# Clustered attention and two feed-forward parts on one core: a new order of the attention steps, with products and sums visited together

## The chip, the cores and the metric
The kernel runs on 1 core of one Trainium2 chip. The metric is the device time of one execution in microseconds (us). PE is the matrix engine, PEld its loading of weights, DVE, ACT and POOL the vector, scalar and GpSimd engines, SP the engine that issues the DMAs here.

## What is computed
```python
# one core computes all of it; B, H, S, D = 2, 8, 768, 64; 16 clusters
q_assign = np.argmax(np.einsum('bhsd,hcd->bhsc', q_n, c_n), axis=-1)   # rows and centroids of length 1
k_assign = np.argmax(np.einsum('bhsd,hcd->bhsc', k_n, c_n), axis=-1)
mask = q_assign[:, :, :, None] == k_assign[:, :, None, :]
scores = np.where(mask, scale * np.matmul(q, k.transpose(0, 1, 3, 2)), -1000000000.0)
attn = np.exp(scores - np.max(scores, axis=-1, keepdims=True))
attn = attn / (np.sum(attn, axis=-1, keepdims=True) + 1e-09)
x = np.matmul(attn, v)              # then laid out as (B*S, H*D) = (1536, 512)
h = x @ w_in                        # first feed-forward part, 2048 wide
x = (np.maximum(h, 0.0) + np.log1p(np.exp(-np.abs(h)))) @ w_out
h = x @ w_in2                       # second one, with a ratio of two polynomials of h
x = (P(h) / (Q(h) + 1e-6)) @ w_out2
```
Where no key has a query's cluster, all scores of that row are equal and the result is the mean of v; the kernel carries such absent rows by a flag.

## The kernel before
The eight pairs of heads (NP = 8) are done in eight steps, `step(j)`, after a lead-in. A step interleaves work of four pairs. Of pair j it does the 24 score products (`scores`, tile `st`: two matrix instructions each, exponential on ACT into `et`, additions of those tiles on POOL into `ea`) and the products with v (`av`: per block of 128 keys two float32 instructions for each half n of the 768 queries, collected in the PSUM banks `av0` and `av1`; in block 0 also one product with `gr` and `gv` for the absent rows). Of pair j+1 it does 24 products for the row maxima (`maxes`, tile `mxs`, each reduced on DVE), then `max_rows1` and `max_rows2` (L293 to L314): DVE takes the larger of two maxima, clips it into `nm` in three operations (the negated maximum, and twice the flag of an absent row), PE transposes `nm` into `nt`, ACT copies it into `nr`, and two DMAs bring its rows into `qt` and `gr`; also the column sums of v (`vsum1` on DVE, `vsum2` on PE). Of pair j+2 it does the transposes of q and k with their split into a high and a low part, the products with the centroids (`dots`, tile `dt`), the one-hot of the nearest centroid (`onehot`, L233 to L252: on DVE a max, a compare, a multiplication on POOL, a min, a compare) and its transposes (`mask_rows`, tile `ot`), whose rows go to `qt` and `kt` by DMA. Of pair j-1 it does the sums of the exponentials (`sums`, tile `sm`, by a product with ones; ACT copies each into SBUF) and `finish` (logarithm and exponential on ACT for the reciprocal, three DVE operations, the high part by ACT and the low part by POOL into `xh` and `xl`).

PSUM has eight banks: `av0`, `av1`, and six that `bank` (L63 to L67) hands out in turn to all other tiles. A product into a bank waits until the tile that had it six calls earlier has been read.

What sets the order is a table, `P["AT"]` (L22): score product i has position i, every other piece of work a position in the table, and `step` writes the pieces in the order of the positions (L695 on). `later` puts off a part of a piece by some places. The lead-in has its own table. In the last step the weights of the feed-forward parts begin to arrive and are decoded on DVE (`decode_w`, four pieces per block, run by `run_pieces`). Behind the steps the last pair's sums are made and finished, and the feed-forward parts follow in units of 512 rows by 128 of the 2048 columns, with four pieces of decoding per unit.

## Time and profile before
| | us |
|---|---|
| median of three runs | 907.64 |
| the three runs | 907.53, 913.1, 907.64 |
| profiled execution, its time | 907.15 |
| profiled execution, its span | 905.4 |
| PE busy | 838.6 (93%) |
| DVE busy | 645.0 (71%) |
| ACT busy | 442.0 (49%) |
| POOL busy | 168.3 (19%) |

The span is what the profile covers, from the first to the last instruction; the execution's own time lies 1.75 us above it. The mean granted clock of PE over the span is 0.962 of full speed. Busy shares are means over parts with different limits, so the stages are read one by one below.

### The profile page before, as it was taken

The numbers are of one execution on the slowest core, as the hardware profiler recorded it, in microseconds if no ns is written. First come the engines' busy times: TensorE is split into PE (matmuls) and PEld (weight loads), VectorE is DVE, ScalarE is ACT, GpSimd is POOL, SyncE is SP. The second block draws the span as 40 slices with busy tenths as digits, with TensorE's granted clock in tenths as the row PEclk, the third lists the DMA queues.
The fourth block names the chain that finished last, engine by engine and source line by source line (L and its number), as shares of the span: only waits on it lengthen the run. The fifth ranks groups of instructions, "written<-read, shape, count | busy, mean of one in ns | idle before, by whom it ended". The sixth has DMA issues, their size and how long they took to land.

```text
span 905.4 us, 10141 instructions
## 1 busy us (share of the span) xinstructions
PE 838.6 (93%) x3721; PEld 612.2 (68%) x3721; DVE 645.0 (71%) x955; ACT 442.0 (49%) x772; POOL 168.3 (19%) x110
## 2 busy tenths in 40 slices
PE   6698898988989967999999999999899999999997
PEld 6565465654645425777888888876678878887885
DVE  6776877868768586887201137887999888888886
ACT  3145354553545534334322233335667776776764
POOL 2063745738458320000000000000000000000000
PEclk9598999999999979999999999999899999999999
DMA  9776364563620729000000005552000010001001
GB/s 195 172 162 146 62 140 89 116 145 77 141 54 12 303 86 401 0 1 1 1 0 1 1 23 209 186 186 93 1 1 1 0 47 1 1 0 47 1 1 47
DMA packets 44290, 71.37 MB, mean 79 GB/s; under 512 B 28320, under 2 KB 30672, under 8 KB 40144
## 3 DMA queue, kind: packets, MB, share of 16 engines
q1 hardware_dynamic: 44240, 70.72, 27.8%
q8 instruction: 29, 0.48, 0.2%
q14 instruction: 21, 0.17, 0.1%
HBM read 43.03 MB, written 3.15 MB: 51 GB/s over the span
## 4 chain that ended last, share of the span: by engine, by line
PE 57%; DVE 28%; ACT 10%; issue 3%; DMA 2%; SPq 0%; DVEq 0%; ACTq 0%
PE av L377 7%; PE h L513 6%; PE h L514 6%; PE h L515 6%; DVE w L474 4%; DVE w L480 4%; PE yp L589 4%; PE yp L590 4%; PE st L351 4%; PE yp L588 4%; PE mxs L283 3%; ACT w L484 3%; PE st L352 3%; DVE w L468 2%; PE yp L585 2%
## 5 line engine op out<-in xcount | busy, mean ns | idle before, releaser
L513 PE MATMUL h<-xh,w 128*128 128x512 f32 x384 | 151.1, 393 | 2.9 <-ACT last L410 2.9
L514 PE MATMUL h<-xl,w 128*128 128x512 f32 x384 | 150.9, 393 | 0.0
L515 PE MATMUL h<-xh,w 128*128 128x512 f32 x384 | 150.8, 393 | 0.0
L356 ACT ACTIVATE et<-st 128x384 f32<-128x384 f32 x192 | 88.6, 488 | 69.3 <-PE st L352 66.0
L289 DVE TENSOR_REDUCE mx<-mxs 128x1 f32<-128x384 f32 x192 | 98.1, 551 | 29.6 <-PE mxs L283 29.5
L362 POOL TENSOR_TENSOR ea<-ea,et 128x768 f32<-128x768 f32 x60 | 109.5, 1844 | 30.7 <-ACT et L356 30.7
L569 DVE TENSOR_TENSOR gl<-y,gh 128x512 fp32r<-128x512 f32 x48 | 33.2, 692 | 96.1 <-ACT gh L561 96.1
L377 PE MATMUL av<-et,vr 128*64 128x384 f32 x384 | 94.0, 565 | 5.8 <-ACT et L356 5.7
L484 ACT CAST w<-w 128x1024 fp32r<-128x1024 f32 x32 | 33.6, 1049 | 124.5 <-DVE w L480 124.5
L513 PEld LDWEIGHTS h<-xh,w 128*128 128x128 f32 x384 | 72.2, 188 | 20.0 <-ACT last L410 3.6
L515 PEld LDWEIGHTS h<-xh,w 128*128 128x128 f32 x384 | 72.2, 188 | 16.5
L514 PEld LDWEIGHTS h<-xl,w 128*128 128x128 f32 x384 | 72.2, 188 | 16.4
L588 PE MATMUL yp<-w,gh 128*128 128x512 f32 x192 | 76.9, 400 | 6.5 <-ACT gh L563 6.3
L585 PE MATMUL yp<-gl,w 128*128 128x512 f32 x192 | 77.6, 404 | 4.1 <-DVE gl L569 4.1
L584 PE MATMUL yp<-gh,w 128*128 128x512 f32 x192 | 76.8, 400 | 3.8 <-ACT gh L561 3.8
L589 PE MATMUL yp<-w,gl 128*128 128x512 f32 x192 | 77.5, 404 | 2.0 <-DVE gl L571 1.9
L590 PE MATMUL yp<-w,gh 128*128 128x512 f32 x192 | 76.3, 397 | 0.0
L586 PE MATMUL yp<-gh,w 128*128 128x512 f32 x192 | 75.5, 393 | 0.0
L351 PE MATMUL st<-qt,kk 128*128 128x384 f32 x192 | 73.6, 383 | 0.0
L526 ACT ACTIVATE y<-h 128x512 f32<-128x512 f32 x48 | 28.5, 594 | 81.9 <-PE h L515 81.8
L283 PE MATMUL mxs<-kt,qt 80*128 80x384 f32 x192 | 63.0, 386 | 5.6 <-DMA kt<-mr 5.6
L352 PE MATMUL st<-qt,kt 81*128 81x384 f32 x192 | 65.9, 343 | 0.0
(140 smaller groups left out, 1452.2 us busy)
## 6 DMA issues: line engine op xcount, KB each, us to landing
w<-in_moe_w SPq DMA_DIRECT2D x32, 1024.0 KB
qt<-hiq SPq DMA_DIRECT2D x16, 384.0 KB
kk<-hik SPq DMA_DIRECT2D x32, 192.0 KB
qraw<-in_q SPq DMA_DIRECT2D x8, 384.0 KB
kraw<-in_k SPq DMA_DIRECT2D x8, 384.0 KB
vr<-in_v SPq DMA_DIRECT2D x8, 384.0 KB
qt<-loq SPq DMA_DIRECT2D x16, 192.0 KB
kt<-hik SPq DMA_DIRECT2D x16, 192.0 KB
```

The lines of the kernel that those rows point to most:

```text
L289: nc.vector.tensor_reduce(out=nm_t[j][:, h, i, n:n + 1], in_=t[:, 0:HS], axis=AX.X, op=ALU.max)
L351: nc.tensor.matmul(t[:, 0:HS], lhsT=KK[j % 2][:, h, c], rhs=QT[j % 3][:, 0, h, r], start=True, stop=False)
L352: nc.tensor.matmul(t[:, 0:HS], lhsT=KT[j % 3][0:65 + C, 1, h, c], rhs=QT[j % 3][0:65 + C, 1, h, r], start=False, stop=True)
L362: eng.tensor_tensor(out=ea[j, h], in0=et[j, 0, h] if first else ea[j, h], in1=e, op=ALU.add)
L377: nc.tensor.matmul(t[64 * h:64 * h + 64, 0:HS], lhsT=VR[j % 2][:, h, kt, :], rhs=et[j, kt, h][:, n, :], start=False, stop=kt == NT - 1,)
L513: nc.tensor.matmul(t, lhsT=wh[:, kk, :], rhs=h, start=kk == 0, stop=False)
L514: nc.tensor.matmul(t, lhsT=wh[:, kk, :], rhs=l, start=False, stop=False)
L515: nc.tensor.matmul(t, lhsT=wl[:, kk, :], rhs=h, start=False, stop=kk == KD - 1)
L585: nc.tensor.matmul(t, lhsT=wh[:, s], rhs=gl, start=False, stop=False)
L588: nc.tensor.matmul(t, lhsT=gh[:, s], rhs=wh, start=first, stop=False)
L589: nc.tensor.matmul(t, lhsT=gl[:, s], rhs=wh, start=False, stop=False)
L590: nc.tensor.matmul(t, lhsT=gh[:, s], rhs=wl, start=False, stop=last)
```

## The change
All steps but the lead-in's get a new table of positions.

- **Joint visits.** `av` is called once per block of keys, for both halves of the queries, as eight or four instructions in a row. The visit to block 0 also makes the sums of the pair before. Its position is 6.6 (before, the two halves had 0.33 and 7.58 behind a block's scores); the last block's is 2.6 in the next step.
- **Sums' banks.** The two `sm` banks are put on the list `held`, which `bank` passes over, until a position behind `finish`. The copies by ACT go for all but the last pair: `finish` now reads and writes the bank itself, adds 1e-9 as a bias of the logarithm and inside its first DVE operation, and stands in three parts at the positions `F`.
- **Maxima.** `max_rows1` is one reduction, which writes the unclipped maxima twice into a tile `mf` that stays (columns 0 to 11 and 32 to 43). PE transposes 44 columns, and DVE clips 12 rows each for the maximum and for the flag out of PSUM. The rows of `gr` are written by two DMAs in place of one.
- **Other positions.** The transposes of q and k stand later, `dots` at 13.8 and 14.8 (before 7.73 and 8.27), `mask_rows` at 19.8 and 20.8 (12.45 and 13.87), `vsum1` at 16.8 (14.74), `vsum2` at 22.5 (46.03), the reading of q and k at 7.5 (16.92). Tiles `ds` and `mr` get buffers of their own.
- **Weights.** Seven and not eight blocks have their place before attention ends, working tiles move to the other pool, and the fourth piece of a decoding is put behind the first of the next.
- **End of attention.** Both halves of `finish` go part by part.

```diff
...
+    AT=dict(MX=[round(0.5 + 0.7 * x, 2) for x in range(24)], AV=6.6, AVP=2.6, T=[-0.5, -0.4, 3.7, 4.7], D=[13.8, 14.8],
+            OT=[19.8, 20.8], F=[8.3, 10.2, 16.4], V1=16.8, V2=22.5, MR=[16.7, 18.6], LK=5.48, LD=7.5, LV=3.2,
+            DE=[15.9, 19.9, 23.9], LAST=8.6, FREE=2.6),
...
-    nbank = [0]
+    nbank, held = [0], []
     def bank(nm):
         nbank[0] += 1
+        while nbank[0] % 6 in held:
...
+    MF = [ap_.tile([128, 2, 32], F32, name=f"mf{s}") for s in range(2)]
...
-        return er_.tile(shape, dt, tag={"ds": "kraw", "mr": "qraw"}.get(tag, tag), name=tag, bufs=bufs)
+        return er_.tile(shape, dt, tag=tag, name=tag, bufs=bufs)
...
     def max_rows1(j):
-        m = nm_t.pop(j)
+        m = nm_t.pop(j).rearrange("p h i n -> p (h i) n")
         assert ("mx", j) in ok
-        nm = nm_p.tile([128, 3, 2 * NT], F32, tag="nm", name="nm", bufs=2)
-        mf = nm_p.tile([128, 2 * NT], F32, tag="mf", name="mf", bufs=2)
-        nc.vector.tensor_reduce(out=mf, in_=m.rearrange("p h i n -> p (h i) n"), axis=AX.X, op=ALU.max)
-        nc.vector.tensor_scalar(nm[:, 0, :], mf, -CLIP, -1.0, op0=ALU.max, op1=ALU.mult)
-        for x in (1, 2):
-            nc.vector.tensor_scalar(nm[:, x, :], mf, -CLIP, None, op0=ALU.is_le)
-        nr_t[j] = nm
+        nc.vector.tensor_reduce(
+            out=MF[j % 2][:, :, 0:2 * NT], in_=m.unsqueeze(1).to_broadcast([128, 2, 2 * NT, 2]), axis=AX.X, op=ALU.max
+        )
     def max_rows2(j):
-        nm = nr_t.pop(j)
         assert j < 2 or ("sm", j - 2) in ok
         ok.add(("mr", j))
         t = bank("nt")
-        nc.tensor.transpose(t[0:36, 0:128], nm.rearrange("p a b -> p (a b)"), ident)
-        nr = nm_p.tile([36, 128], F32R, tag="nr", name="nr", bufs=2)
-        nc.scalar.copy(nr, t[0:36, 0:128])
-        move(QT[j % 3][64 + C:65 + C, 1, :, :], nr[0:12, :])
-        move(GR[j % 2], nr[12:36, :])
+        w = 32 + 2 * NT
+        nc.tensor.transpose(t[0:w, 0:128], MF[j % 2].rearrange("p a b -> p (a b)")[:, 0:w], ident)
+        nr = nm_p.tile([w, 128], F32R, tag="nr", name="nr", bufs=2)
+        nc.vector.tensor_scalar(nr[0:2 * NT, :], t[0:2 * NT, 0:128], -CLIP, -1.0, op0=ALU.max, op1=ALU.mult)
+        nc.vector.tensor_scalar(nr[32:w, :], t[32:w, 0:128], -CLIP, None, op0=ALU.is_le)
+        move(QT[j % 3][64 + C:65 + C, 1, :, :], nr[0:2 * NT, :])
+        for x in range(2):
+            move(GR[j % 2][2 * x:2 * x + 2], nr[32:w, :])
...
-    def av(j, kt, n):
-        if kt == 0:
-            av_t[j, n] = ps1.tile([128, 512], F32, tag=f"av{n}", name="av")
-        t = av_t[j, n]
-        r = slice(n * HS, (n + 1) * HS)
+    def av(j, kt, p=None):
+        if p is not None:
+            for n in range(2):
+                sm_t[p, n] = bank("sm")
+                held.append(nbank[0] % 6)
+                absent(sm_t[p, n], p, n, g768[64 * (p % 2):64 * (p % 2) + 4, :])
         if kt == 0:
             assert ("gv", j) in ok
-            nc.tensor.matmul(t[:, 0:HS], lhsT=GV[j % 2], rhs=GR[j % 2][:, r], start=True, stop=False)
-        for h in range(2):
-            nc.tensor.matmul(
-                t[64 * h:64 * h + 64, 0:HS], lhsT=VR[j % 2][:, h, kt, :], rhs=et[j, kt, h][:, n, :],
-                start=False, stop=kt == NT - 1,
-            )
-        if n == 1 and kt == NT - 1:
+            for n in range(2):
+                av_t[j, n] = ps1.tile([128, 512], F32, tag=f"av{n}", name="av")
+                absent(av_t[j, n], j, n, GV[j % 2])
+        if p is not None:
+            sums(p)
+        for n in range(2):
+            for h in range(2):
+                nc.tensor.matmul(
+                    av_t[j, n][64 * h:64 * h + 64, 0:HS], lhsT=VR[j % 2][:, h, kt, :], rhs=et[j, kt, h][:, n, :],
+                    start=False, stop=kt == NT - 1,
+                )
+        if kt == NT - 1:
             ok.add(("av", j))
-        if n == 1 and kt != 0:
+        if kt != 0:
             for h in range(2):
                 et.pop((j, kt, h))
         if kt == NT - 1 and j < NP - 1:
-            evac_av(j, n, nm_p.tile([128, HS], F32, tag=f"avs{n}", name="avs"))
+            for n in range(2):
+                evac_av(j, n, nm_p.tile([128, HS], F32, tag=f"avs{n}", name="avs"))
+    def absent(t, j, n, g):
+        nc.tensor.matmul(t[:, 0:HS], lhsT=g, rhs=GR[j % 2][:, n * HS:(n + 1) * HS], start=True, stop=False)
     def evac_av(j, n, t):
         avs_t[j, n] = t
         nc.scalar.activation(out=t, in_=av_t.pop((j, n))[:, 0:HS], func=AF.Copy, scale=-1.0)
-    def sums(j, n):
-        t = bank("sm")
-        r = slice(n * HS, (n + 1) * HS)
-        p = 64 * (j % 2)
-        nc.tensor.matmul(t[:, 0:HS], lhsT=g768[p:p + 4, :], rhs=GR[j % 2][:, r], start=True, stop=False)
-        for h in range(2):
-            nc.tensor.matmul(
-                t[64 * h:64 * h + 64, 0:HS], lhsT=ones, rhs=ea[j, h][:, n, :], start=False, stop=True
-            )
-        if n == 1:
-            ea.pop((j, 0)), ea.pop((j, 1))
-            ok.add(("sm", j))
-        sm_t[j, n] = t
-        if j < NP - 1:
-            evac_sums(j, n, nm_p.tile([128, HS], F32, tag="sm", name="sm", bufs=2))
+    def sums(j):
+        for n in range(2):
+            for h in range(2):
+                nc.tensor.matmul(
+                    sm_t[j, n][64 * h:64 * h + 64, 0:HS], lhsT=ones, rhs=ea[j, h][:, n, :], start=False, stop=True
+                )
+        ea.pop((j, 0)), ea.pop((j, 1))
+        ok.add(("sm", j))
     def evac_sums(j, n, sm):
-        nc.scalar.activation(out=sm, in_=sm_t[j, n][:, 0:HS], func=AF.Identity, bias=eps9)
+        nc.scalar.activation(out=sm, in_=sm_t[j, n][:, 0:HS], func=AF.Copy)
         sm_t[j, n] = sm
-    def finish(j, n, d1=P["DF"][0], d2=P["DF"][1]):
-        sm = sm_t.pop((j, n))
-        r0 = fin.tile([128, HS], F32, tag="r0", name="r0")
-        nc.scalar.activation(out=r0, in_=sm, func=AF.Ln)
-        nc.scalar.activation(out=r0, in_=r0, func=AF.Exp, scale=-1.0)
-        r = slice(j // PB * S + n * HS, j // PB * S + (n + 1) * HS)
-        hi, lo = xh[j % PB][:, r], xl[j % PB][:, r]
-        a = avs_t.pop((j, n))
-        def rest():
-            nc.vector.tensor_tensor(out=sm, in0=sm, in1=r0, op=ALU.mult)
-            nc.vector.scalar_tensor_tensor(out=r0, in0=sm, scalar=-2.0, in1=r0, op0=ALU.add, op1=ALU.mult)
-            nc.vector.tensor_tensor(out=a, in0=a, in1=r0, op=ALU.mult)
-        def last():
+    r_t = {}
+    def finish(j, n, part):
+        sm = sm_t[j, n] if j == NP - 1 else sm_t[j, n][:, 0:HS]
+        if part == 0:
+            r_t[j, n] = fin.tile([128, HS], F32, tag="r0", name="r0", bufs=2)
+        r0, a = r_t[j, n], avs_t[j, n]
+        if part == 0:
+            nc.scalar.activation(out=r0, in_=sm, func=AF.Ln, bias=eps9)
+            nc.scalar.activation(out=r0, in_=r0, func=AF.Exp, scale=-1.0)
+        elif part == 1:
+            nc.vector.scalar_tensor_tensor(out=sm, in0=sm, scalar=EPS, in1=r0, op0=ALU.add, op1=ALU.mult)
+            nc.vector.scalar_tensor_tensor(out=sm, in0=sm, scalar=-2.0, in1=r0, op0=ALU.add, op1=ALU.mult)
+            nc.vector.tensor_tensor(out=a, in0=a, in1=sm, op=ALU.mult)
+        else:
+            r = slice(j // PB * S + n * HS, j // PB * S + (n + 1) * HS)
+            hi, lo = xh[j % PB][:, r], xl[j % PB][:, r]
             nc.scalar.copy(hi, a)
             nc.gpsimd.tensor_tensor(out=lo, in0=a, in1=hi.bitcast(F32), op=ALU.subtract)
-        later(d1, rest)
-        later(d2, last)
+            sm_t.pop((j, n)), r_t.pop((j, n)), avs_t.pop((j, n))
...
+    NA = 7
...
-        return pools["wa" if s < 8 else "wb"].tile([128, 2 * NW], dt, tag=f"w{s}", name=f"w{s}")
+        return pools["wa" if s < NA else "wb"].tile([128, 2 * NW], dt, tag=f"w{s}", name=f"w{s}")
...
-        pieces.extend(((f, c), x) for x in (first, second, third, fourth))
+        key = (f, c)
+        pieces.extend([(key, first)] + tail + [(key, second), (key, third)])
+        tail[:] = [(key, fourth)]
     def run_pieces(n=0, upto=None):
-        while pieces and (n > 0 or upto and pieces[0][0] <= upto):
-            pieces.pop(0)[1]()
+        while True:
+            todo = pieces or tail
+            if not todo or not (n > 0 or upto and todo[0][0] <= upto):
+                return
+            todo.pop(0)[1]()
...
-        return pools["wb"].tile([128, TB], dt, tag=nm, name=nm, bufs=bufs)
+        return pools["wa"].tile([128, TB], dt, tag=nm, name=nm, bufs=bufs)
...
+            put(at["AVP"], lambda: av(prev, NT - 1), prev is not None)
+            for kt in range(NT - 1):
+                put(4 * kt + at["AV" if m is not None else "LAST"], lambda kt=kt: av(main, kt, prev if kt == 0 else None))
             for n in range(2):
-                put(at["AVP"][n], lambda n=n: av(prev, NT - 1, n), prev is not None)
-                for kt in range(NT - 1):
-                    put(4 * kt + 4 + at["AV"][n], lambda kt=kt, n=n: av(main, kt, n))
                 for w in range(2):
                     put(at["T"][2 * w + n], lambda w=w, n=n: transposes(p, "qk"[w], n), p is not None and p > 2)
                 put(at["D"][n], lambda n=n: dots(p, n), p is not None)
                 put(at["OT"][n], lambda n=n: mask_rows(p, n), p is not None)
-                put(at["SM"][n], lambda n=n: (sums(prev, n), finish(prev, n)), prev is not None)
+                for x in range(3):
+                    put(at["F"][x] + n + (0 if m is not None else at["LAST"] - at["AV"]), lambda n=n, x=x: finish(prev, n, x), prev is not None)
+                put(at["F"][1] + n + at["FREE"], lambda: held.pop(0), prev is not None)
...
-        for c in range(8):
+        for c in range(NA):
             stage_w(0, c)
         step(NP - 1)
-        av(NP - 1, NT - 1, 0)
-        av(NP - 1, NT - 1, 1)
+        av(NP - 1, NT - 1)
         for n in range(2):
-            sums(NP - 1, n)
+            sm_t[NP - 1, n] = bank("sm")
+            absent(sm_t[NP - 1, n], NP - 1, n, g768[64 * ((NP - 1) % 2):64 * ((NP - 1) % 2) + 4, :])
+        sums(NP - 1)
...
-        for n in range(2):
-            finish(NP - 1, n, 1, 2)
-            tick(), tick()
-        for c in range(8, KF - 2):
+        for x in range(3):
+            for n in range(2):
+                finish(NP - 1, n, x)
+        for c in range(NA, KF - 2):
```

In the order of PE, a middle step (score products of pair 3) around the sums of the pair before; `st` are score products, `mxs` those of the maxima, `sm` the sums, `av` the products with v. Before:
```order
L397 MATMUL sm<-gr,g_76 128x384
L399 MATMUL sm<-ea,ones 64x384 x2
L351 MATMUL st<-qt_100,kk_107 128x384
L352 MATMUL st<-qt_100,kt_103 128x384
L283 MATMUL mxs<-kt_104,qt_101 128x384
L351 MATMUL st<-qt_100,kk_107 128x384
L352 MATMUL st<-qt_100,kt_103 128x384
L375 MATMUL av<-gr,gv 128x384
L377 MATMUL av<-et,vr_109 64x384 x2
L351 MATMUL st<-qt_100,kk_107 128x384
L352 MATMUL st<-qt_100,kt_103 128x384
L397 MATMUL sm<-gr,g_76 128x384
```
After, the joint visit of the same step:
```order
L290 MATMUL mxs<-kt_104,qt_101 128x384
L402 MATMUL sm<-gr,g_76 128x384 x2
L402 MATMUL av<-gr,gv 128x384 x2
L411 MATMUL sm<-ea,ones 64x384 x4
L388 MATMUL av<-et,vr_109 64x384 x4
L290 MATMUL mxs<-kt_104,qt_101 128x384
L355 MATMUL st<-qt_100,kk_107 128x384
L356 MATMUL st<-qt_100,kt_103 128x384
```
The three visits to the sums and to `av`, which stood between score products, have become one stretch of twelve instructions with the sums of both halves in it.

In the order of DVE, behind the products with the centroids; `ds` and `dmx` belong to the one-hot, `mx` and `mf` to the maxima, `vs` to the column sums of v. Before:
```order
L227 TENSOR_REDUCE ds<-dt 128x192 x2
L241 TENSOR_REDUCE dmx<-ds 128x24
L242 TENSOR_TENSOR ds<-ds,dmx 128x384
L289 TENSOR_REDUCE mx<-mxs 128x1 x3
L246 TENSOR_REDUCE dmx<-ds 128x24
L249 TENSOR_TENSOR ds<-iota,dmx 128x384
L289 TENSOR_REDUCE mx<-mxs 128x1 x4
L320 TENSOR_REDUCE vs<-vr_108 128x128
```
After, in the same step:
```order
L234 TENSOR_REDUCE ds<-dt 128x192
L296 TENSOR_REDUCE mx<-mxs 128x1
L234 TENSOR_REDUCE ds<-dt 128x192
L248 TENSOR_REDUCE dmx<-ds 128x24
L249 TENSOR_TENSOR ds<-ds,dmx 128x384
L296 TENSOR_REDUCE mx<-mxs 128x1 x3
L302 TENSOR_REDUCE mf_112<-mx 128x2x12
L324 TENSOR_REDUCE vs<-vr_108 128x128
L253 TENSOR_REDUCE dmx<-ds 128x24
L256 TENSOR_TENSOR ds<-iota,dmx 128x384
L313 TENSOR_SCALAR nr<-nt 12x128
L314 TENSOR_SCALAR nr<-nt 12x128
```
The reduction into `mf` and the column sums of v stand ahead of the last two operations of the one-hot, and the two clips, now on `nr`, behind them.

In the order of PE, the end of a step; `nt` is the transpose of the maxima, `tp` that of q and k, `vt` the column sums, `ot` the transposes of the one-hot. Before:
```order
L351 MATMUL st<-qt_102,kk_106 128x384
L352 MATMUL st<-qt_102,kt_105 128x384
L351 MATMUL st<-qt_102,kk_106 128x384
L352 MATMUL st<-qt_102,kt_105 128x384
L377 MATMUL av<-et,vr_108 64x384 x2
L309 MATMUL nt<-ident,nm 36x128
L377 MATMUL av<-et,vr_108 64x384 x2
L327 MATMUL vt<-vs,ones 2x128
L164 MATMUL tp<-ident,qraw 128x128 x6
L377 MATMUL av<-et,vr_108 64x384 x4
```
After, in the same part of the step:
```order
L355 MATMUL st<-qt_100,kk_107 128x384
L356 MATMUL st<-qt_100,kt_103 128x384
L388 MATMUL av<-et,vr_109 64x384 x4
L311 MATMUL nt<-ident,mf_112 44x128
L355 MATMUL st<-qt_100,kk_107 128x384
L356 MATMUL st<-qt_100,kt_103 128x384
L267 LDWEIGHTS ds
L267 MATMUL ot<-ident_70,ds 64x128
L267 LDWEIGHTS ds
L267 MATMUL ot<-ident_70,ds 64x128
```
The transpose `nt`, which stood between products with v behind the last score product, stands behind a whole visit and ahead of the transposes `ot`, with a score product between.

## Rows read from the trace of the kernel before

**Rows 1.** Windows: us, busy time by engine, granted clock, DMA share, GB/s.
```profile
153.00:191.00 38.00, 34.54 (x179) 21.00 (x177) 28.82 (x49) 18.93 (x42) 21.72 (x13) 0.95 0.52 112
427.00:546.00 119.00, 118.78 (x515) 96.34 (x514) 25.44 (x35) 32.60 (x54) 0.00 (x0) 1.00 0.04 14
```
**Rows 2.** Waits: engine and line that waited, for whom, us in total, times, longest.
```profile
PE nt L309 <- DVE nm L301: 21.2, 8, 2.7
PE ot L260 <- DVE ds L249: 4.2, 5, 0.9
```
**Rows 3.** Timeline from 183 to 188 us: start, duration, engine, line, out<-in, idle before.
```profile
183.59 3.56 POOL L362 TENSOR_TENSOR ea<-ea,et 128x768 f32<-128x768 f32 x2 [1.20 <-ACT et L356]
183.94 1.49 DVE L299 TENSOR_SCALAR nm<-mf 128x12 f32<-128x12 f32 x1
185.34 1.85 DVE L301 TENSOR_SCALAR nm<-mf 128x12 f32<-128x12 f32 x2
187.24 0.29 PE L309 MATMUL nt<-ident,nm 128*36 128x128 f32 x1 [2.63 <-DVE nm L301]
```
**Rows 4.** Timeline of DVE at the end of the lead-in, the first clip.
```profile
40.37 0.17 DVE L299 TENSOR_SCALAR nm<-mf 128x12 f32<-128x12 f32 x1
```
**Rows 5.** Windows of 2 to 6 us, each just behind a hole of PE.
```profile
72.00:78.00 6.00, 5.75 (x19) 2.39 (x21) 2.30 (x7) 1.58 (x4) 0.16 (x1) 0.50 0.02 5
188.00:191.50 3.50, 3.50 (x15) 1.76 (x14) 1.95 (x6) 0.98 (x2) 0.00 (x0) 0.52 0.02 5
332.00:334.00 2.00, 2.00 (x7) 0.82 (x6) 2.00 (x3) 0.17 (x1) 0.00 (x0) 0.50 0.00 0
340.00:342.00 2.00, 2.00 (x9) 1.64 (x10) 0.57 (x2) 1.33 (x3) 0.00 (x0) 1.00 1.04 426
```
**Rows 6.** Timeline of PE in a middle step, score products and products with v.
```profile
196.20 0.34 PE L351 MATMUL st<-qt,kk 128*128 128x384 f32 x1
196.38 0.33 PE L352 MATMUL st<-qt,kt 81*128 81x384 f32 x1
196.64 0.43 PE L375 MATMUL av<-gr,gv 4*128 4x384 f32 x1
197.00 0.87 PE L377 MATMUL av<-et,vr 128*64 128x384 f32 x4
197.80 0.44 PE L351 MATMUL st<-qt,kk 128*128 128x384 f32 x1
198.08 0.34 PE L352 MATMUL st<-qt,kt 81*128 81x384 f32 x1
```
**Rows 7.** Timelines of DVE, PE and ACT in the last step and behind it.
```profile
323.25 2.30 DVE L468 TENSOR_SCALAR w<-w 128x1024 uint32<-128x1024 uint32 x1
331.09 3.58 PE L377 MATMUL av<-et,vr 128*64 128x384 f32 x8 [2.16 <-ACT et L356]
339.97 0.50 PE L513 MATMUL h<-xh,w 128*128 128x512 f32 x1 [2.93 <-ACT last L410]
346.75 0.51 ACT L429 CAST xh<-last 128x384 fp32r<-128x384 f32 x1 [2.09 <-DVE last L426]
```
**Rows 8.** Timeline of DVE behind the second products with the centroids, a middle step.
```profile
205.56 0.55 DVE L241 TENSOR_REDUCE dmx<-ds 128x24 f32<-128x384 f32 x1
206.15 0.56 DVE L242 TENSOR_TENSOR ds<-ds,dmx 128x384 f32<-128x384 f32 x1
206.63 1.48 DVE L289 TENSOR_REDUCE mx<-mxs 128x1 f32<-128x384 f32 x3
208.02 0.54 DVE L246 TENSOR_REDUCE dmx<-ds 128x24 f32<-128x384 f32 x1
208.59 1.44 DVE L249 TENSOR_TENSOR ds<-iota,dmx 128x384 bf16<-128x384 f32 x1
```
**Rows 9.** Lines: the column sum of v on DVE; busy time, mean ns, idle before.
```profile
L320 DVE TENSOR_REDUCE vs<-vr 128x128 f32<-128x768 f32 x8 | 12.1, 1510 | 0.0
```
**Rows 10.** One line's instructions, the one-hot: shortest, median and longest in ns.
```profile
L249 DVE TENSOR_TENSOR ds<-iota,dmx x8: 557/1436/1448, 18.6 to 246.4; 128x384 bf16<-128x384 f32 x8
```

More of the change, by code (lines that the diff above doesn't have):

```diff
@@ L19 @@
 CLIP = float(2.0 ** 60)
-P = dict(LAG=6, I0=2, L=[0, 2, 3, 4], FIN=[8, 12], ORD='gi s0 ev e4 e3 de e2 e1 s1 go', DT=1, DD=1, DO=8, DF=[4, 13],
-    AT=dict(MX=[0.52, 3.72, 5.26, 5.34, 8.39, 9.39, 10.39, 12.2, 12.32, 13.64, 14.24, 14.86, 15.36, 16.01, 16.53, 17.43, 18.38, 19.03, 19.11, 19.77, 20.02, 20.08, 20.12, 21.64], AV=[0.33, 7.58], AVP=[-3.07, -1.36], T=[-6.73, -5.56, -0.01, 0.51], D=[7.73, 8.27], OT=[12.45, 13.87], SM=[2.92, 5.06], V1=14.74, V2=46.03, MR=[21.65, 26.91], LK=5.48, LD=16.92, LV=-1.25, DE=[15.9, 19.9, 23.9], SP=[19.95, 23.95]),
+P = dict(DT=1, DD=1, DO=8,
+    AT=dict(MX=[round(0.5 + 0.7 * x, 2) for x in range(24)], AV=6.6, AVP=2.6, T=[-0.5, -0.4, 3.7, 4.7], D=[13.8, 14.8],
+            OT=[19.8, 20.8], F=[8.3, 10.2, 16.4], V1=16.8, V2=22.5, MR=[16.7, 18.6], LK=5.48, LD=7.5, LV=3.2,
+            DE=[15.9, 19.9, 23.9], LAST=8.6, FREE=2.6),
     LEAD=dict(CT=-3.26, T0=[0, 1, 2, 3], D0=[3.54, 4.41], T1=[5.03, 6.13, 7.03, 7.96], O0=[9.69, 10.33], D1=[9.44, 10.44], O1=[16.53, 19.95], T2=[42.38, 43.88, 44.05, 46.48], MX=[12.1, 13.1, 14.1, 15.08, 16.1, 17.1, 18.1, 19.1, 20.1, 21.1, 22.1, 23.1, 24.1, 25.1, 26.1, 27.1, 28.1, 29.1, 30.1, 31.1, 32.1, 33.1, 34.1, 35.1], C2=5.33, LK=15.05, LD=0.75, V1=9.2, V2=10.7, MR=[36.3, 36.83], DO=[4, 0], MV=[16.86, 22.72]))
@@ L62, in clustered_attention_two_ffns @@
     ps1 = ctx.enter_context(tc.tile_pool(name="ps1", bufs=1, space=bass.MemoryType.PSUM))
-    nbank = [0]
+    nbank, held = [0], []
     def bank(nm):
         nbank[0] += 1
+        while nbank[0] % 6 in held:
+            nbank[0] += 1
         return ps1.tile([128, 512], F32, tag=f"s{nbank[0] % 6}", name=nm)
@@ L208, in clustered_attention_two_ffns @@
     ds_t, oh_t = {}, {}
+    EPS = 1e-9
     NX = HH * 4
@@ L450, in stage_w @@
         nc.sync.dma_start(out=wt[f, c], in_=(w1, w2)[f][c].bitcast(U32))
-    pieces = []
+    pieces, tail = [], []
     def decode_w(f, c):
@@ L620, in clustered_attention_two_ffns @@
         eps9 = const.tile([128, 1], F32, name="eps9")
-        nc.vector.memset(eps9, 1e-9)
+        nc.vector.memset(eps9, EPS)
         one = const.tile([128, 1], F32, name="one")
@@ L639, in clustered_attention_two_ffns @@
         nc.gpsimd.memset(gv.bitcast(F32), 0.0)
+        for s in range(2):
+            nc.gpsimd.memset(MF[s], 0.0)
         csq = er_.tile([128, D], F32, name="csq")
```

1 line of the change is left out of this document (removed).

## The prediction
> **What bounds the kernel now.** I read the stages first. In a middle attention step the matrix engine (PE) is busy for 34.54 of 38 us and its granted clock is only 0.95, while DVE has 28.8 us of work and ACT 18.9; in the feed-forward part that follows PE is busy 118.78 of 119 us at clock 1.00 [rows 1]. So the attention steps are PE's, with holes in them, and the next thing to read is who makes the holes. The list of waits names two: PE waits 21.2 us in 8 places for the clipped maxima before their transpose `nt`, and 4.2 us in 5 places for the one-hot masks before `ot` [rows 2]. The timeline of the end of a step shows the first of them: after the last maximum DVE clips 12 numbers per partition in three small operations that take 1.49 and 1.85 us (for two), and PE stands still for 2.63 us [rows 3]. In the lead-in, where POOL has nothing to do, the first of these operations took 0.17 us [rows 4]; in the step a pair of POOL additions ran beside them and ended at 183.59 + 3.56 = 187.15, 0.04 before they did. [...] A step therefore loses 2.65 + 0.84 us of waiting (21.2 / 8 and 4.2 / 5) and 3.5 x 0.48 = 1.7 us of clock.
>
> The profiled execution took 907.15 us, its span is 905.4; the median of the three runs is 907.64. I sum against 907.15 and take the result as it stands.
>
> **What goes.** (a) The transpose of the maxima now stands behind a joint visit of eight product instructions and takes the raw maxima; on DVE only one reduction (some 0.2 us, after the 0.17 of rows 4) lies between the last maximum and it. The clips follow it, on 12 rows of 128 out of PSUM; no row shows them, the nearest are the clip's own 0.17 alone and 1.49 beside POOL. I take 0.3 each, and at either price they stand behind what PE waits for. So the wait goes in steps 0 to 6: 7 x 2.65 = 18.5 us. In the lead-in PE waits for the queue of maxima, not for the clips, so there it stays, less some 0.3.
> (b) The half clock behind it: 3.0 us in step 0 (72 to 78), 1.7 in each of six other steps, 13.2 us.
> (c) PE work. A score product starts 0.18 us after the one before; going into a float32 product costs 0.26, the first score behind it 0.28, and the single mask product of 4 rows 0.36 [rows 6]. Each float32 instruction takes 0.20 (four in 0.80). The number of them is unchanged. By the order, a step had 13 stretches of float32 work and now has 11 (products that already stood beside transposes gain nothing): 2 x 0.19; and of four single mask products three no longer stand alone: 3 x 0.18. That is 0.9 us a step, 6.5 in seven.
> (d) At the end of attention ACT did logarithm and exponential of the second half only after it had waited for DVE's first half; its last copy waited 2.09 us for DVE [rows 7]. Now both halves go ahead: 1.9 us, and the feed-forward part starts that much earlier.
> Together 40.1 us.
>
> At nothing I count: the dropped copies of the sums and of `nr` on ACT (an engine busy 18.93 of 38 us), the reads of q and k issued earlier, one more small transfer per step, and the new list of weight pieces: four pieces are run per unit as before, and DVE's order there is the same. ACT's idle half and DMA queues busy 0.52 of the stage [rows 1] cover these; if that fails the price is some tenths of a us per step.
>
> **What comes.** (e) The sums' two banks leave the rotation of six from the joint visit until DVE has finished with each. I count from the start of that visit. PE: 4 mask products and 16 float32 instructions, 4.1 us; then to the 20th maximum 11 max products, 7 score pairs and a visit of eight, 1.96 + 2.5 + 1.8 = 6.3, in all 10.4. DVE gets the first of these maxima at 4.5 and must do seven maxima at 0.49 (three in 1.48 [rows 8]) and six operations of the finish at 0.57: 4.5 + 6.9 = 11.4. The 20th maximum uses the second sums' bank, so PE waits 1.0; I add 0.7 for the dots behind it, which wait for the 17th maximum, and for smaller waits of the kind. I take 1.7 us, between 0 (if DVE overlaps better) and 2.5. The finish reads and writes PSUM in place; that form has no row. The bounds are the 0.56 of the compare and the 1.44 of the one-hot [rows 8], both two-operand operations of its size; I take 0.57.
> In steps 1 to 6: 10.2 us.
> (f) The masks. Behind the reduction of the second dots DVE had max, compare, three maxima, min, one-hot: 205.56 to 210.03 [rows 8], and PE waited 0.84. Now the dots come eight positions later in the step, and between the three maxima and the min stand the reduction of the maxima and the column sum of v, 1.51 us [rows 9]. The new chain: 0.55 + 0.55 + 0.56 + 1.48 + 0.2 + 1.51 + 0.54 + (0.56 to 1.45) = 5.95 to 6.84, with the small gaps 6.0 to 6.9, starting 0.3 behind PE's last dot. PE has five score pairs, three max products, one visit of eight, `nt`: 1.8 + 0.5 + 1.8 + 0.4 = 4.5. So PE waits 1.9 to 2.8 us at `ot`. There is one thing more: the compare starts about 1.5 us after the last dot, and POOL's addition of the scores just released (1.78 us, half of the pair of rows 3) about 1.4 after it. The one-hot, of the same kind, took 0.56 at best, in the lead-in, and 1.45 at most, beside a POOL addition [rows 10]; the compare of rows 8 had none beside it. If it is held like that, the chain grows by 1.6 and PE waits 3.8 in two parts (at `nt`, then at `ot`). I take 3.3 us, nearer to the second; the ends are 1.9 and 4.4. Six steps, less the 4.2 us of today: 15.6 us.
> [...]
> (g) A hole of this size lowers the clock or not: those at `nt` did, one of 2.16 did (0.50 behind it), one of 2.93 did not (1.00) [rows 5, 7]; those of 0.84 did not, since 3.5 us at 0.52 alone make the mean of 0.95 in 38 us. I take three in four: 6 x 0.75 x 1.7 = 7.7 us.
> (h) In the last step POOL's two subtractions of the finish move from before the weight decode into it; a decoding operation that ran beside POOL took 2.30 us [rows 7]. I take one such operation as the cost, against a start some 1.1 earlier: 1.2, bounds -1 and 3.
> Together 34.7 us.
>
> **Sum.** 907.15 - 40.1 + 34.7 = 901.7, say 902 us. The wait moves from the maxima to the masks, and most of the gain is spent there.
>
> **Rivals.** *The wait at the masks stays short and the clock full.* [...] Against it: the column sum's 1.5 us is certain, and 2.16 was enough once. Then (e) 1.0 x 6, (f) 2.0 x 6 - 4.2, (g) and (h) nothing: 13.8 added, 881 us.
> *Slower: the compare is held behind POOL in each masked step.* Place: DVE's compare behind the second dots. It costs the top of (f), 4.4 x 6 - 4.2 = 22.2; the split wait leaves PE so little to do that the clock stays low as long as after 72 us, 3.0 x 6 = 18; the late DVE stretches (e) to 2.5, 15.0, and (h) is 2.3: 57.5 added, 924.5 us. It decides from the point where (e), (f) and (g) add 6.7 us per step. For it: POOL is first by 0.1 us in my count. Against it: only one of seven holes had the long low clock.
> [...]
>
> **How the numbers follow.** A measurement of this kernel can tell about 1%, 9 us, from no change. My forecast (waits traded, 895 to 909) has 0.50, the first rival 0.34, the slower one 0.14, and 0.02 is left. Faster by over 1% (under 898) takes the first rival and the lower end of mine: 0.43. Within 1%: 0.43. Slower: 0.14. The range reaches from the first rival's 882 to 913, which leaves out most of the slower one and the last of the faster.
>
> **What would show it.** Right: no wait of PE at `nt` in the waits beyond some tenths, or 1.6 us where the compare is held; a wait of 2 to 4 us at `ot` behind the one-hot in six places; DVE busy without a gap from the joint visit to the second finish, and max products or dots waiting about 1 us there for DVE; the clock at 0.5 for some 3 us behind `ot`; a step with no masks to wait for (the seventh) shorter by some 4 us. Wrong: `ot` waits under 1.5 us and the clock of a middle step is 1.00 (then the first rival), or a middle step is over 39 us (then the slower one); or the feed-forward part, which I leave untouched, differs by more than 3 us.

## Result and the profile after

The changed kernel is slower: a median of 924.46 us in 20 executions (913.55 to 931.68) against 908.53 in 20 of the kernel before, and a ratio of 1.011 between comparable executions (interval 1.008 to 1.014); the comparisons leave disturbed runs out. The forecast was 902, with a range up to 913. The profiled execution took 921.84 us, 14.7 more than the one before.

First the stages, as windows from one step's first score product to the next one's (columns as in [rows 1]). Of the kernel before, a middle step and the last:

```profile
117.02:154.84 37.82, 34.32 (x181) 20.98 (x179) 28.83 (x49) 18.99 (x42) 21.72 (x13) 0.95 0.51 112
299.46:339.97 40.51, 31.79 (x120) 15.10 (x118) 27.89 (x24) 18.77 (x40) 11.82 (x6) 0.86 0.55 221
```

Of the changed kernel, the same two, and the step without masks:

```profile
121.52:162.70 41.18, 36.54 (x181) 23.03 (x179) 25.86 (x48) 17.62 (x39) 21.30 (x13) 0.88 0.50 104
283.38:312.15 28.77, 27.75 (x137) 17.10 (x137) 19.06 (x37) 14.82 (x32) 17.05 (x11) 0.93 0.16 42
312.15:354.84 42.69, 28.41 (x128) 15.33 (x127) 28.52 (x26) 18.38 (x40) 16.65 (x9) 0.88 0.48 192
```

A middle step is 3.4 us longer. PE stands still for 41.18 - 36.54 = 4.64 us in place of 3.50, 1.1 more. The clock costs 41.18 x 0.12 = 4.9 us in place of 37.82 x 0.05 = 1.9, 3.0 more. What is left, PE's work at full clock, falls from 32.4 to 31.6. So the joint visits do save work (0.8 us), holes change little, and the clock takes more than three times what the visits save. Steps 1 to 5 together are 14.9 us longer; by the same reckoning the clock (0.88, in step 3 0.91; before 0.95) costs 23.2 us in them in place of 9.4, 13.8 more. Step 0 is 0.9 shorter, the step without masks 3.5 shorter, the last 2.2 longer, and the lead-in 2.1. The feed-forward part begins 14.87 us later (354.84 against 339.97) and then takes as long as before.

The waits of PE (columns as in [rows 2]), of the changed kernel:

```profile
PE ot L267 <- DVE ds L256: 12.9, 6, 2.9
PE nt L311 <- DVE mf L302: 11.9, 7, 2.4
...
PE mxs L290 <- DVE avs L435: 6.1, 6, 1.0
...
PE st L355 <- DVE avs L435: 4.9, 2, 3.4
```

The 21.2 us at `nt` [rows 2] have become 11.9, `ot` has gone from 4.2 to 12.9, and two lines are new: maxima and scores that wait for DVE's finish of the sums, whose banks are kept out. DVE, step 1 of the changed kernel, in order of time:

```profile
91.68 2.58 DVE L296 TENSOR_REDUCE mx<-mxs 128x1 f32<-128x384 f32 x5 [2.96 <-PE mxs L290]
94.17 0.56 DVE L433 SCALAR_TENSOR_TENSOR sm<-sm,r 128x384 f32<-128x384 f32 x1
94.77 0.57 DVE L434 SCALAR_TENSOR_TENSOR sm<-sm,r 128x384 f32<-128x384 f32 x1
...
98.16 0.56 DVE L435 TENSOR_TENSOR avs<-avs,sm 128x384 f32<-128x384 f32 x1
...
108.68 2.15 DVE L249 TENSOR_TENSOR ds<-ds,dmx 128x384 f32<-128x384 f32 x1
...
112.26 0.20 DVE L302 TENSOR_REDUCE mf<-mx 128x24 f32<-128x48 f32 x1
112.38 1.49 DVE L324 TENSOR_REDUCE vs<-vr 128x128 f32<-128x768 f32 x1
...
114.36 0.74 DVE L256 TENSOR_TENSOR ds<-iota,dmx 128x384 bf16<-128x384 f32 x1
```

and POOL and PE beside it:

```profile
108.57 1.83 POOL L366 TENSOR_TENSOR ea<-ea,et 128x768 f32<-128x768 f32 x1 [8.04 <-ACT et L360]
...
98.86 0.41 PE L290 MATMUL mxs<-kt,qt 80*128 80x384 f32 x1 [0.96 <-DVE avs L435]
112.52 0.29 PE L311 MATMUL nt<-ident,mf 128*44 128x128 f32 x1 [1.58 <-DVE mf L302]
115.15 0.35 PE L267 MATMUL ot<-ident,ds 128*64 128x128 bf16 x3 [1.99 <-DVE ds L256]
```

During the joint visit DVE has nothing for 2.96 us, then maxima and finish together; PE waits 0.96 for the finish. The compare starts 0.11 us behind POOL's addition and takes 2.15 us in place of 0.56. In windows, the clock behind the first dots of step 1, behind `ot` in step 1, behind the first dots of step 2, and behind those of step 3, where it held:

```profile
99.00:106.00 7.00, 7.00 (x27) 4.36 (x27) 2.69 (x6) 0.49 (x1) 1.53 (x1) 0.54 0.26 43
117.00:120.00 3.00, 3.00 (x10) 0.95 (x11) 1.73 (x4) 1.06 (x3) 2.52 (x2) 0.50 0.20 35
140.00:147.00 7.00, 6.93 (x25) 4.32 (x25) 2.90 (x6) 0.49 (x1) 1.68 (x1) 0.54 0.19 31
182.00:188.00 6.00, 6.00 (x43) 4.80 (x43) 3.32 (x8) 1.15 (x3) 1.09 (x2) 1.00 0.04 8
```

So there are two stretches of low clock (0.54 and 0.50 over the windows above) in steps 1, 2, 4 and 5, one behind the first dots and one behind `ot`, together some 10 us; in step 3 there is only the second. Before there was one, of some 3.5 us behind `nt` [rows 5].

### The profile page after: what moved, and what is told of

The parts are those of the page before. It is cut to its first block, busy times and chain, and to the rows that moved or that the text cites. A ratio compares the mean times of both kernels' runs of the same rounds, so it can differ in the third digit from the quotient of the medians.

```text
span 920.1 us, 10156 instructions
## 1 busy us (share of the span) xinstructions
PE 841.7 (91%) x3721; PEld 623.1 (68%) x3721; DVE 627.3 (68%) x947; ACT 433.2 (47%) x750; POOL 166.0 (18%) x112
## 4 chain that ended last, share of the span: by engine, by line
PE 61%; DVE 26%; ACT 9%; DMA 2%; issue 2%; SPq 1%; DVEq 0%; ACTq 0%
PE av L388 7%; PE h L528 6%; PE h L529 6%; PE h L530 6%; DVE w L489 4%; DVE w L483 4%; PE st L355 4%; PE yp L604 4%; PE yp L605 4%; PE yp L603 4%; PE mxs L290 4%; ACT w L493 3%; PE st L356 3%; PE dt L227 3%; DVE w L477 2%; PE yp L600 2%
## 5 line engine op out<-in xcount | busy, mean ns | idle before, releaser
L360 ACT ACTIVATE et<-st 128x384 f32<-128x384 f32 x192 | 91.9, 491 | 140.7 <-PE st L356 138.2
L296 DVE TENSOR_REDUCE mx<-mxs 128x1 f32<-128x384 f32 x192 | 96.6, 550 | 41.8 <-PE mxs L290 41.3
L584 DVE TENSOR_TENSOR gl<-y,gh 128x512 fp32r<-128x512 f32 x48 | 33.2, 693 | 96.6 <-ACT gh L576 96.6
L388 PE MATMUL av<-et,vr 128*64 128x384 f32 x384 | 87.9, 584 | 5.8 <-ACT et L360 5.8
L355 PE MATMUL st<-qt,kk 128*128 128x384 f32 x192 | 80.5, 419 | 5.0 <-DVE avs L435 4.9
L290 PE MATMUL mxs<-kt,qt 80*128 80x384 f32 x192 | 65.6, 393 | 14.2 <-DMA kt<-mr 8.1
L356 PE MATMUL st<-qt,kt 81*128 81x384 f32 x192 | 70.1, 365 | 0.0
```

The lines of the kernel that those rows point to most:

```text
L290: nc.tensor.matmul(t[:, 0:HS], lhsT=QT[j % 3][0:64 + C, 1, h, i * 128:(i + 1) * 128], rhs=KT[j % 3][0:64 + C, 0, h, n * HS:(n + 1) * HS], ...
L296: nc.vector.tensor_reduce(out=nm_t[j][:, h, i, n:n + 1], in_=t[:, 0:HS], axis=AX.X, op=ALU.max)
L355: nc.tensor.matmul(t[:, 0:HS], lhsT=KK[j % 2][:, h, c], rhs=QT[j % 3][:, 0, h, r], start=True, stop=False)
L356: nc.tensor.matmul(t[:, 0:HS], lhsT=KT[j % 3][0:65 + C, 1, h, c], rhs=QT[j % 3][0:65 + C, 1, h, r], start=False, stop=True)
L388: nc.tensor.matmul(av_t[j, n][64 * h:64 * h + 64, 0:HS], lhsT=VR[j % 2][:, h, kt, :], rhs=et[j, kt, h][:, n, :], start=False, stop=kt == N ...
```

## Experiments

### Which part earns: the clip alone
The kernel before with the new `max_rows1`, `max_rows2` and `mf`, nothing else.

> The kernel before with one part of the change alone: maxima transposed unclipped, clipped on DVE out of the transposed rows. Theory: the wait of 2.65 us at the transpose goes in seven steps (18.5 us) with the half clock behind it (13 us), and the masks' chain is as before: 876 us, the granted clock of a middle step 1.00. Rival (the time is needed elsewhere, the maxima themselves or the DMA of the rows come late): the wait moves to the first score products of the next step, 890 to 905 us.

Measured: 886.32 us median, 875.86 in the profiled execution; ratio 0.967 (0.957 to 0.976). A middle step, and the only wait left in it:

```profile
106.90:140.49 33.59, 32.74 (x181) 20.27 (x179) 26.78 (x49) 18.66 (x41) 21.76 (x13) 1.00 0.58 128
...
124.34 0.35 PE L262 MATMUL ot<-ident,ds 128*64 128x128 bf16 x3 [0.85 <-DVE ds L251]
```

In the profiled execution the theory holds to the microsecond: a middle step falls from 37.82 to 33.59, the clock is at 1.00. The other three executions took 882.36 to 891.95 us and have no trace. Terms (a) and (b) of the prediction were right for the clip; some 30 us were to be had (3.3% by the ratio), and the rest of the change gave them back and more.

### The late masks alone on top of the clip

```diff
-    D=[7.73, 8.27], OT=[12.45, 13.87]
+    D=[13.8, 14.8], OT=[19.8, 20.8]
...
-        tag={"ds": "kraw", "mr": "qraw"}.get(tag, tag)
+        tag=tag
```

> The kernel before with two parts of the change: the clip, and the late place of the dots (13.8, 14.8) and of the masks' transposes (19.8, 20.8), with buffers of their own for them; the products with v stay split and the sums are copied by ACT. In all runs with joint visits so far the clock fell to 0.5 behind the first dots, even where the hole there was filled. Theory one (the joint visits do it): behind the dots the clock stays at 1.00, and only the masks' rows come late for the first maximum of the next step, some 1.6 us in six places, with 1.7 of clock behind each at most: against the clip alone (875.9 in its undisturbed execution) 886 to 896 us. Theory two (the late dots do it, with DVE late at them): the clock falls there too: 900 us or more.

Measured: 891.49 us median, 882.04 profiled; ratio 0.984 (0.978 to 0.990).

```profile
111.37:145.32 33.95, 33.35 (x180) 20.49 (x179) 26.54 (x49) 18.79 (x41) 21.73 (x13) 1.00 0.61 127
...
136.49 0.44 PE L285 MATMUL mxs<-kt,qt 80*128 80x384 f32 x1 [0.60 <-DVE mx L291]
```

The step grows by 0.36 us and the clock stays at 1.00, behind the dots too. So the late dots alone did not lower it in this execution; it is the shortest of four, and the other three (888.01 to 897.76 us) have no trace. The masks' rows did not come late here.

### The joint products without the sums
The clip, the end of attention part by part, later masks, and both halves of `av` at the second one's position; sums apart, copied by ACT. The run after it is the same without the joint positions.

```diff
-    AV=[0.33, 7.58], AVP=[-3.07, -1.36]
+    AV=[7.57, 7.58], AVP=[-1.37, -1.36]
```

> The kernel before with the clip of the change, the end part by part, the masks' transposes later, and the joint visits of the change for the products with v alone (both halves at the position of the second; the sums stay apart with their copies). Theory: PE's work in a middle step falls from 32.8 to some 31.6 us (five stretches of float32 work fewer, 0.2 each, and the mask products side by side) with no new wait: against the run with the same edits but split visits (882.0 us median) 7 us less, 875; in an undisturbed execution 868. Rival (denser PE work brings a hole at the score or maximum products, as DVE and ACT are fed in bursts): 882 us or more, with waits of PE for DVE's maxima.

> The kernel before with the clip of the change, the end of attention done part by part for both halves (with two buffers for the reciprocal), and the transposes of the masks 1.75 positions later (14.2 and 15.6). Theory: against the run of the clip alone (875.9 in its profiled execution) the five waits of 0.84 us for the one-hot go (4.2 us) and the end saves 1.9: 870 us. Rival (the rows of the masks then arrive late for the maxima of the next step): 876 us or more.

Measured: joint 905.63 us, ratio 0.994 (0.991 to 0.997); split 881.99, ratio 0.966 (0.960 to 0.972). The joint one:

```profile
115.83:156.58 40.75, 38.71 (x181) 25.09 (x179) 27.36 (x48) 18.76 (x41) 22.13 (x13) 0.79 0.49 105
128.00:144.00 16.00, 15.63 (x46) 9.29 (x47) 9.76 (x16) 4.59 (x9) 9.41 (x6) 0.50 0.17 40
...
128.37 0.69 PE L350 MATMUL st<-qt,kk 128*128 128x384 f32 x1 [1.95 <-DVE ds L229]
```

PE waits less than 2.1 us in this step, but behind the one hole of 1.95 us the clock stands at 0.50 for 16 us. Joint visits, with neither the late dots nor the banks kept out, take back 2.8 of the 3.4% that the split version had gained. The rival held, with the dots' reduction in place of the maxima. That the hole lowers the clock here is not shown: in the profiled execution of the split run it fell twice for as long, right behind the dots and with no hole (last section). In the split run the waits at `ot` are gone, but its median cannot be told from that of the clip alone, and the end part by part gained nothing: from the last visit of `av` to the first product of the feed-forward part it is 8.89 us in both (299.72 to 308.61, 313.93 to 322.82).

### The hole in front of the dots, filled

```diff
+        if x == 18 and j >= 2:
+            for _ in range(5):
+                nc.tensor.matmul(
+                    t[:, 0:HS], lhsT=QT[j % 3][0:64 + C, 1, h, i * 128:(i + 1) * 128],
+                    rhs=KT[j % 3][0:64 + C, 0, h, n * HS:(n + 1) * HS], start=True, stop=True,
+                )
```

> The changed kernel; the 19th product for the maxima, the last one ahead of the wait for the sums' banks, is done six times in place of once in steps 1 to 6 (the same values into the same bank; 5 x 0.18 = 0.9 us), so that PE works in the hole of 1.03 us and waits some 0.1. No wait of another engine changes. Theory (the clock pays for the hole): the half clock behind the first dots goes, 11.7 us in the profiled execution, the hole's own time stays: 910 us. Rival (the clock falls there because of the dense visits ahead, whatever PE does in the hole): 922 us with 0.5 behind the dots as before.

Measured: 915.78 us, ratio 1.003 (1.000 to 1.007) against the changed kernel's 1.011. Steps 1 and 3, and the clock behind the first dots of step 3:

```profile
87.34:126.05 38.71, 35.02 (x185) 22.43 (x184) 25.86 (x48) 17.73 (x39) 21.33 (x13) 0.91 0.54 110
...
165.53:206.56 41.03, 37.27 (x186) 23.32 (x184) 25.82 (x48) 17.84 (x39) 21.30 (x13) 0.88 0.51 104
...
185.50:188.50 3.00, 3.00 (x13) 1.76 (x14) 1.37 (x3) 0.49 (x1) 0.17 (x1) 0.55 0.04 9
```

Work that computes nothing new made the kernel faster by 0.8%: in steps 1 and 2 the stretch is gone and the step some 2 us shorter. In step 6, which has no dots and no masks, it is gone too; first the changed kernel there, behind its hole of 1.02 us, then the kernel with the hole filled:

```profile
302.00:304.00 2.00, 2.00 (x7) 0.76 (x8) 0.84 (x2) 0.49 (x1) 0.18 (x1) 0.50 0.00 0
```

```profile
300.00:312.00 12.00, 11.87 (x61) 7.49 (x62) 10.37 (x21) 6.69 (x16) 9.12 (x7) 1.00 0.00 0
```

In steps 3 to 5 it is there all the same, with PE idle for no more than 0.2 us ahead of it. The profiled execution was the longest of eleven (925.93 us), so others may have had fewer such stretches. So the theory is half right: the hole is one cause of the lower clock, not the only one. Of two kernels with dots at the same place, the one with split visits did not show it in its profile and this one did; what in the joint visits does it, these runs leave open.

### DVE's part of the finish later

```diff
-    F=[8.3, 10.2, 16.4]   DO=8
+    F=[8.3, 12.6, 16.4]   DO=9
```

> The changed kernel with DVE's part of the finish 2.4 positions later (12.6 and 13.6; the banks are given back as much later), so that eleven maxima and not seven stand ahead of it. In the trace DVE has 5.8 us idle between the dots. Theory (the half clock behind the first dots comes from the 1.03 us hole): hole and stretch go in steps 1 to 6, 6.2 and 11.7 us: 904 us. Rival (the clock falls there for another reason, the dense visits): only the hole goes, 916 us, and the clock is 0.5 behind the dots as before. Second rival (the finish now delays the dots' reductions and the chain to the masks): no change or slower, 922 us and above.

Measured: 911.15 us, ratio 1.002 (0.998 to 1.005) against the changed kernel's 1.011. The 1.03 us at the sums' banks go, but with the banks kept out longer a score product then waits for maxima:

```profile
121.00:159.77 38.77, 35.13 (x180) 21.50 (x179) 25.75 (x48) 17.64 (x38) 21.31 (x13) 0.91 0.54 110
...
149.60 0.44 PE L355 MATMUL st<-qt,kk 128*128 128x384 f32 x1 [2.19 <-DVE mx L296]
```

Between the first theory and the rival in time, and neither in kind: the hole moved.

### Copies of the sums by ACT

```diff
-                held.append(nbank[0] % 6)
...
+            for n in range(2):
+                evac_sums(p, n, nm_p.tile([128, HS], F32, tag="sm", name="sm", bufs=2))
```

In all steps, and in the last alone:

> The changed kernel, but ACT copies the sums out of their banks right behind the joint visit, and the banks stay in the rotation. Theory (the clock pays for the holes): the changed kernel waits 1.03 us for the sums' banks in each of steps 1 to 6, and behind most of these holes the clock stands at 0.5; with the hole the clock loss behind it goes too. Sum from its profiled 921.84: holes 6 x 1.03 = 6.2, their clock loss about 11.7, the last step's two waits for the same banks 4.9 with 3.0 of clock: about 896 us. Rival (the clock falls for other reasons, as the denser visits): only the holes go, 911 us, and the clock is still 0.5 behind the first dots. Second rival (DVE is late anyway, the wait moves to the dots): 918 us or more.

> The changed kernel, but in the last step the sums of the pair before are copied by ACT and their banks stay in the rotation. Theory: PE's two waits for DVE's finish there (1.48 and 3.40 us) and the half clock behind the second (3.0 us) go: 914 us. Rival (DVE's finish beside POOL takes longer out of SBUF, as in the run with all copies, and PE waits for maxima or exponentials in its place): 919 to 925 us.

Measured: 944.34 us in all steps, ratio 1.038 (1.032 to 1.045), the worst of all runs; 919.94 in the last step alone, ratio 1.011 (1.005 to 1.017), no change from the changed kernel. With all copies:

```profile
139.31 2.07 DVE L435 SCALAR_TENSOR_TENSOR sm<-sm,r 128x384 f32<-128x384 f32 x1
141.48 1.97 DVE L436 TENSOR_TENSOR avs<-avs,sm 128x384 f32<-128x384 f32 x1
...
139.11 3.93 POOL L366 TENSOR_TENSOR ea<-ea,et 128x768 f32<-128x768 f32 x2 [0.25 <-ACT et L360]
...
143.97 0.69 PE L355 MATMUL st<-qt,kk 128*128 128x384 f32 x1 [2.77 <-DVE mx L296]
```

With all copies the first theory and its rival failed; DVE is late, as the second rival had it, but more than that, and for a reason that none named. Out of SBUF and beside POOL the finish's operations take 2.07 and 1.97 us; in place in PSUM all 42 of them took 0.55 to 0.57. The banks kept out are the cheaper way once the visits are joint. In the last step the rival held: the two waits of 1.48 and 3.40 us went and one of 4.51 for the exponentials came.

### The chain to the masks
The column sum behind the one-hot; the dots one position earlier; that and the masks earlier with a later first maximum; and all edits together.

```diff
-    V1=16.8
+    V1=21.5
-    D=[13.8, 14.8]
+    D=[12.8, 13.8]
-    OT=[19.8, 20.8], MX=[round(0.5 + 0.7 * x, 2) for x in range(24)]
+    OT=[18.9, 19.9], MX=[round(1.9 + 0.64 * x, 2) for x in range(24)]
```

> The changed kernel with the column sum of v issued behind the one-hot in place of ahead of it (position 21.5 for 16.8); nothing else. The chain to the one-hot loses 1.5 us. Theory: PE's wait at the transposes of the masks falls from 2.0 to 0.5 us in five steps and from 2.9 to 1.4 in one, 9 us in all, and part of the 16.5 us of half clock behind it goes: 905 us, 896 if all of it goes. Rival (the wait goes to the product of the column sums, which stands some 2 us behind): 918 to 922 us, with a wait of over 1 us there.

> The changed kernel with both products with the centroids one position earlier (12.8 and 13.8), sums still in the banks kept out. In the trace of the changed kernel the one-hot's compare starts 0.1 us behind POOL's addition and takes 2.15 us in place of 0.56. Theory: one position earlier it runs ahead of POOL, and PE's waits at nt and ot (3.58 us in five steps, 4.6 in one: 22.5 us) go with the half clock behind them (16.5): 883 us if the wait for the sums' banks stays as it is. Rival (DVE is then late at the dots, as in the run with all three edits, where PE waited 2.75 us there and the clock stood at 0.5 for 10 us): 910 to 925 us.

> The run with the dots one position earlier, where PE's last wait in a middle step was 1.8 us for the masks' rows at the first maxima of the next step; here the masks' transposes stand 0.9 positions earlier and the first maximum 1.4 later. Theory (the clock pays for holes): that wait shrinks under 0.5 us and the half clock behind it goes: from 904.8 less 6 x 1.6 less 6 x 1.7 = 885 us. Rival (the maxima, now in a shorter space, wait for DVE): 900 us or more.

> The changed kernel with the copies by ACT, the column sum behind the one-hot, and both products with the centroids one position earlier, so that the compare of the one-hot starts before POOL's addition and not behind it. Theory: no wait over 0.5 us is left for PE in a middle step and the clock stays at 1.00: from 921.8 less 25.7 (copies) less 3.6 x 6 (nt and ot) less 16.5 of clock: about 858 us. Rival (the compare is held wherever it stands, or the clock falls for another reason than the holes): 885 us or more.

Measured: column sum late 920.16 us, ratio 1.014 (1.006 to 1.022); dots early 904.76, 0.993 (0.991 to 0.996); masks early too 897.80, 0.987 (0.984 to 0.991); all with the copies 926.92, 1.017 (1.009 to 1.025). With the column sum late, DVE and POOL:

```profile
158.59 2.14 DVE L256 TENSOR_TENSOR ds<-iota,dmx 128x384 bf16<-128x384 f32 x1
...
158.51 1.80 POOL L366 TENSOR_TENSOR ea<-ea,et 128x768 f32<-128x768 f32 x1
...
160.78 0.35 PE L267 MATMUL ot<-ident,ds 128*64 128x128 bf16 x3 [1.97 <-DVE ds L256]
```

The chain lost 1.5 us, so the one-hot started 0.08 us behind the next addition and took 2.14 in place of 0.74: PE waits 1.97 as before. The rival had the time, not the place. The compare of the changed kernel is the same case. It started 0.11 us behind a POOL addition of 1.83, took 2.15 and ended 0.43 behind the addition's end (108.68 + 2.15 and 108.57 + 1.83); the one-hot here ended 0.42 behind it (158.59 + 2.14 and 158.51 + 1.80). What held the two, these runs do not show.

With the dots one position earlier the waits at `nt` and `ot` are all but gone in steps 1 to 5 (one of 0.52 us is left), as the theory said, and the hole at the sums' banks too; the time came out between theory and rival. One reason is a new wait, for the masks' rows; first with the dots alone, then with the masks earlier:

```profile
151.42 0.41 PE L290 MATMUL mxs<-kt,qt 80*128 80x384 f32 x1 [1.81 <-DMA kt<-mr]
```

```profile
143.40:181.01 37.61, 34.89 (x181) 21.54 (x179) 27.76 (x49) 17.31 (x39) 21.36 (x14) 0.91 0.55 114
...
145.77 0.41 PE L290 MATMUL mxs<-kt,qt 80*128 80x384 f32 x1 [1.42 <-DMA kt<-mr]
```

The hole shrank from 1.8 to 1.4 and not under 0.5, and the clock stays at 0.91 in the mean; the time lies between theory and rival again. The other reason is the clock behind the dots. In the run with the dots alone, ahead of the second dots of step 2, behind them, and behind the hole of 1.81 us:

```profile
121.00:133.50 12.50, 12.24 (x67) 7.63 (x67) 9.26 (x19) 5.67 (x12) 7.38 (x5) 1.00 1.11 220
135.00:140.00 5.00, 5.00 (x16) 2.57 (x16) 2.14 (x4) 0.49 (x1) 1.16 (x2) 0.50 0.02 3
152.00:170.00 18.00, 17.55 (x97) 11.17 (x95) 12.78 (x26) 9.57 (x21) 7.76 (x5) 1.00 1.02 217
```

It fell at the dots, where PE had stood still for no more than 0.23 us at a time, and held behind the hole of 1.81. The same happened at the dots in all of steps 1 to 5 of both runs, with no stop of PE over 0.32 us in the 14 us ahead. So with joint visits the clock can fall at the dots where no hole stands. With all edits, where the rival held, PE waited 2.75 us at the dots for maxima that stood behind a finish out of SBUF:

```profile
140.17 0.30 PE L227 MATMUL dt<-cc,hiq 128*128 128x64 f32 x1 [2.75 <-DVE mx L296]
```

## Why the prediction was wrong

- (a) and (b), the clip: right in themselves, as the clip alone shows. The 1.7 us of clock a step are 3.5 x 0.48 of the line of 188.00 to 191.50 in [rows 5]. In the changed kernel 1.58 us stay at `nt`, the split wait that the prediction named for a held compare.
- (c) the joint visits' work: 0.9 us a step forecast, 32.4 - 31.6 = 0.8 measured.
- (d) 1.9 us at the end: nothing, since the first product of the feed-forward part waits for the copies of the last sums by ACT in both kernels (2.93 us before [rows 7], 3.6 after), and not for the finish.
- (e) 1.7 us at the sums' banks: 1.03. The finish in PSUM at 0.57 was right.
- (f) 3.3 us at the masks: 1.58 + 1.99 = 3.57, with the compare held at 2.15 us as in the upper case.
- (g) is the step that failed: "A hole of this size lowers the clock or not", counted for the holes at the masks alone and at 6 x 0.75 x 1.7 = 7.7 us for all of them. The waits of a middle step came nearly as forecast: (e) and (f) make 1.03 + 3.57 = 4.60 us, for 5.0. The clock costs 4.9 us there, not 1.3, with two stretches in most steps, one behind the masks and one behind the first dots. The holes of 0.96 to 1.03 us at the sums' banks were priced by their length, since those of 0.84 had left the clock alone (1.00 from 96.6 to 100 us of the kernel before); and with joint visits the clock fell at the dots without a hole too (three steps with the hole filled, steps 1 to 5 with the dots early). In steps 1 to 5 the clock was to cost 2 us less than before and cost 13.8 more, most of the 20 us between the sum of 901.7 and the profiled 921.84. Why the clock stood lower with these joint visits (0.88 in a middle step, before 0.95) stays open.
- (h) 1.2 us in the last step: that step is 2.2 longer. The two waits of 4.9 us for the same banks were not in the sum; there DVE does some of the additions too, and the second half's finish stands behind one that waits for the exponentials of the scores.
- The lead-in's 2.1 us were not forecast, and belong to no part of the change that the runs could show: with the same lead-in the first step began at 42.77 us in one profile and at 45.50 in another.

The slower rival had the place right (the compare behind POOL in the masked steps) and its sum of 924.5 is near the measured time, but by other prices, so the nearness is partly luck: (f) 3.57 for its 4.4, (e) 1.03 for its 2.5, and 4.9 of clock in a middle step for its 3.0. The sign that the prediction gave for it, a middle step over 39 us, came (41.18). Its chance of 0.14 rested on "only one of seven holes had the long low clock", a count from a schedule with other work around its holes.

## What to carry to other kernels

Take a change apart before it is judged: here one edit of a dozen lines was worth 3.3%, and lay under a new schedule that cost more than that. Joining PE's visits saved 0.8 us of work on PE in a middle step, but left DVE idle for 2.96 us in step 1 and then busy without a gap for 8.9 (91.68 to 98.63 + 1.95), so count the partner's queue behind each joint visit. Do not price the clock by the length of holes alone: here it held behind one of 1.81 us (1.00) and fell where PE had stood still for no more than 0.23 at a time (0.50). Where DVE works beside POOL, ask of each operation whether POOL's next one starts just ahead of it (0.11 us ahead the compare took 2.15 us for 0.56, 0.08 ahead the one-hot 2.14 for 0.74): a chain that is shortened by 1.5 us can gain nothing.

The two best versions, the clip alone and the clip with the end part by part and later masks, both beat the kernel before (ratios 0.967 and 0.966) and cannot be told apart.
